# A mixture of experts, dense and then sparse: gathers issued one block earlier, the last six tiles routed as one batch, an accumulator's pool closed inside the last step, and gate scaling at other points

## The chip, the cores and the metric

The kernel runs on one core of a Trainium2 chip. The metric is the time of one execution on the device, in microseconds (us): 2072.86 us is the median of three runs of the kernel before. The engines are named PE (TensorE), DVE (VectorE), ACT (ScalarE), POOL (GpSimd) and SP (SyncE, which only issues transfers and register work here). Each engine executes its own list of instructions in order; waits between engines go by semaphores.

## What is computed

Three parts, all in float32: linear attention over 4 x 8 heads of 576 positions, a dense mixture of experts whose gate is balanced by eight Sinkhorn rounds, and a sparse mixture in which each of 2304 rows goes to one of eight experts.

```
# x: [2304, 512] from the attention
logits = x @ w_gate;  P = exp(logits - logits.max())
for _ in range(8):                       # Sinkhorn
    P /= P.sum(1, keepdims=True) + 1e-9
    P /= P.sum(0, keepdims=True) + 1e-9
    P *= N / E
x = sum(P[:, e:e+1] * (relu(x @ w1[e]) @ w2[e]) for e in range(8))
# sparse: the nearest expert by cosine
logits = normalize(x) @ normalize(expert_emb).T / tau
probs = softmax(logits);  idx = argmax(logits, axis=1)
out[idx == e] = probs[idx == e, e] * (relu(x[idx == e] @ w1b[e]) @ w2b[e])
```

## The kernel before

A product in float32 is made of three float32r matmuls: each operand is split into a high part (a cast) and a low part (the difference), and high x high, high x low and low x high are summed. The casts are mostly ACT's (L328, L374, L456, L926), the differences DVE's or POOL's (L329, L457, L927).

**Stage 1** (to about 290 us) is the attention. **Stage 2** (to about 1753 us) is the dense mixture, 24 steps: an expert e and a block bi of 768 rows (`ORDER`). A step has two groups g, halves of the hidden features. A group is 14 products (`p1_group`, matmuls L447 to L449 into psA, a Strassen-like scheme with seven products for each of two halves j) and then six tiles of the second layer (`p2_tile`, matmuls L668 to L670 into psD), whose results DVE adds into `acca` and `accb`, scaled by the gate. psA has four places. In a half, ACT copies the first product to tu (L469), and later casts h1h (L456, from tv) and h0h (L456), from which DVE makes h1l and h0l (L457). A place of psA comes free when its low part is made.

The work that is laid beside this is placed by hand. A group's 14 products and 6 tiles are its **ticks** 0 to 19. `at_tick(step, g, tick, fn)` puts a function behind a tick; ticks above 19 in the lists of the last steps mean the next group. Placed so are: `w1_tasks(e, g)`, which prepares w1 of an expert (six functions: casts on ACT and subtractions on POOL by `wpiece`, L328 and L329, with POOL's sums L345, L350, L354 and L360 between them); `w2_task`; the routing of the sparse mixture; and the first loads of stage 3. The gate (`gate_logits`) and its Sinkhorn rounds (`sinkhorn`) are generators in a list of hooks; `hook()` advances one of them by a piece. Before, that happens behind each odd tick, from step 0 on behind every one. A Sinkhorn round ends in column sums: DVE makes cs (L650), PE sums over the partitions (L653).

**Routing.** A batch of three tiles of 128 rows goes through `route_a` (squares, transposes L715), `route_l` (logits L725), `route_b` (the best expert on DVE, from L733), `route_c` (ranks, L752 and L753), `route_s`, `route_d` (slot numbers, L768 to L774), `route_w` (weight, and the write of the rows to the DRAM table x2d, L784) and `route_i`: one scatter by POOL for each tile, which writes the row numbers to the tables ids (L788). There are three tables, one for each place in a batch; a scatter waits for the landing of the scatter before it into the same table. Batches 0 and 3 (named by their first tile) lie in step 22, 6 and 9 in step 23, and the last six tiles, which come last out of the accumulator `accb`, are batches 12 and 15.

**Stage 3** is a loop over 22 blocks of 128 places (`second`), each of one expert. `load_ids(i)` loads a block's row numbers (SP: table reads L877 to L879 and three transfers idr from ids, L890), `gather(i)` adds them up (POOL, L897 to L899) and gathers the rows xgs (POOL, L901) into one of two places; `tx` transposes them (L935, ACT's xth L938, DVE's xtl L939 and gt L941), `p1` multiplies by w1 (L955 to L957), `th_` transposes h (L970), `p2` multiplies by w2 (L988 to L990), and the output is scattered by POOL (L994). `wcond` loads a quarter of an expert's matrix where the expert changes (SP, L906), and `wsplit` makes its parts: the casts on ACT (L926), for the last quarter of w2 on POOL (L924), and the low parts on DVE (L927). The first `NEARLY` blocks are known after twelve tiles (`first_blocks`), the others after all (`other_blocks`, a generator).

## Time and profile before

| | us |
|---|---|
| runs | 2067.79, 2072.86, 2074.79 |
| median | 2072.86 |
| the profiled execution, its own time | 2069.92 |
| its span, first to last instruction | 2067.9 |
| PE busy | 2017.4 (98%) |
| DVE busy | 1101.6 (53%) |
| ACT busy | 723.9 (35%) |
| POOL busy | 584.1 (28%) |

The mean granted clock of TensorE is 0.994 of full speed. The profiled execution lies 2.94 us below the median, and its span leaves 2.0 us outside. A share of busy time is a mean over the three stages; what matters is where an engine waits and for what, so the rows below are cut by stretches. A group's line reads "line engine operation output<-input, count | busy us, mean ns | idle time before it and what ended it"; a wait's line "us in total, times, longest".

### The profile page before, as it was taken

Reading aid. Unit: us, or ns where it says so; the run is one execution under the profiler, and the core shown is the slowest. Engines: PE = TensorE matmul, PEld = TensorE weight load, DVE = VectorE, ACT = ScalarE, POOL = GpSimd, SP = SyncE. Lnnn points to the kernel's source line nnn. Section 1 sums busy time; section 2 is a strip of 40 time slices with the busy share of each in tenths; the row PEclk is TensorE's granted clock in tenths of the full one; section 3 lists DMA queues with packets and bytes.
Section 4 is the critical chain, followed back from the end, with each engine's and each line's share of the span. In section 5 each row is a group of like instructions: output and inputs, shape, how many; then the busy total and the mean of one; then the engine's idle time right before and its main releaser. Section 6 shows DMA issues by size and latency. Waiting matters only on the chain.

```text
span 2067.9 us, 28848 instructions
## 1 busy us (share of the span) xinstructions
PE 2017.4 (98%) x10947; PEld 1814.6 (88%) x10947; DVE 1101.6 (53%) x1994; ACT 723.9 (35%) x1331; POOL 584.1 (28%) x482
## 2 busy tenths in 40 slices
PE   9999999999999999999999999999999999799898
PEld 8999888888988998998998998998998988687776
DVE  6766443654444444444444444444444546888886
ACT  5566433321231122113212311321231223687775
POOL 1246452420050034006102400420050102456553
PEclk9999999999999999999999999999999999999999
DMA  3344343112213111221302222112212537252851
GB/s 115 113 142 168 112 166 122 42 42 107 107 62 127 74 54 61 107 107 42 125 31 100 82 107 107 41 57 91 107 62 107 44 106 113 56 204 78 308 189 43
DMA packets 76671, 208.32 MB, mean 101 GB/s; under 512 B 18272, under 2 KB 37984, under 8 KB 76530
## 3 DMA queue, kind: packets, MB, share of 16 engines
q1 hardware_dynamic: 72434, 195.94, 29.0%
q0 software_dynamic: 4096, 10.51, 1.6%
q8 instruction: 87, 1.43, 0.3%
q14 instruction: 54, 0.44, 0.1%
HBM read 230.00 MB, written 31.99 MB: 127 GB/s over the span
## 4 chain that ended last, share of the span: by engine, by line
PE 79%; DVE 6%; DMA 4%; POOL 4%; issue 3%; ACT 2%; SPq 1%; POOLq 0%; DVEq 0%; ACTq 0%
PE psD L668 12%; PE psD L669 12%; PE psD L670 12%; PE psA L447 11%; PE psA L449 11%; PE psA L448 11%; PE psD L197 3%; DMA idr<-ids 2%; POOL xgs L901 2%; DVE s2l L927 2%; DVE s1l L927 1%; PE psB L168 1%; PE psC L168 1%; DMA rw<-in_moe_w 1%; POOL s2h L924 1%
## 5 line engine op out<-in xcount | busy, mean ns | idle before, releaser
L329 POOL TENSOR_TENSOR wA<-raw,wA 128x512 fp32r<-128x512 f32 x48 | 60.9, 1295 | 805.2 <-ACT wA L328 805.2
L679 DVE SCALAR_TENSOR_TENSOR acca<-psD,Pm,acca 128x512 f32<-128x512 f32 x168 | 126.2, 751 | 280.5 <-PE psD L670 279.4
L668 PE MATMUL psD<-w2h,h0h 128*128 128x512 f32 x576 | 225.7, 392 | 0.5 <-DVE accb L679 0.5
L669 PE MATMUL psD<-w2h,h0l 128*128 128x512 f32 x576 | 224.4, 390 | 0.6 <-DVE h0l L457 0.6
L669 PE MATMUL psD<-w2h,h1l 128*128 128x512 f32 x576 | 224.4, 390 | 0.0
L670 PE MATMUL psD<-w2l,h0h 128*128 128x512 f32 x576 | 224.3, 389 | 0.0
L668 PE MATMUL psD<-w2h,h1h 128*128 128x512 f32 x576 | 224.1, 389 | 0.0
L670 PE MATMUL psD<-w2l,h1h 128*128 128x512 f32 x576 | 224.1, 389 | 0.0
L469 ACT COPY tu<-psA 128x384 f32<-128x384 f32 x96 | 46.0, 479 | 446.5 <-PE psA L449 446.5
L447 PE MATMUL psA<-xT,wS 128*128 128x384 f32 x576 | 194.6, 338 | 0.0
L448 PE MATMUL psA<-xT,wS 128*128 128x384 f32 x576 | 192.6, 334 | 0.0
L449 PE MATMUL psA<-xT,wS 128*128 128x384 f32 x576 | 192.5, 334 | 0.0
L456 ACT ACTIVATE h1h<-tv 128x384 fp32r<-128x384 f32 x96 | 50.4, 525 | 264.6 <-DVE tv L461 264.6
L457 DVE SCALAR_TENSOR_TENSOR h0l<-psA,h0h 128x384 fp32r<-128x384 f32 x192 | 106.5, 555 | 62.2 <-ACT h0h L456 61.9
L456 ACT ACTIVATE h0h<-psA 128x384 fp32r<-128x384 f32 x192 | 94.4, 491 | 112.8 <-DVE psA L461 105.9
L679 DVE SCALAR_TENSOR_TENSOR accb<-psD,Pm,accb 128x512 f32<-128x512 f32 x84 | 63.1, 751 | 132.6 <-PE psD L670 121.0
L447 PE MATMUL psA<-xB,wA 128*128 128x384 f32 x384 | 129.9, 338 | 0.0
L927 DVE TENSOR_TENSOR s2l<-rw,s2h 128x1024 fp32r<-128x1024 f32 x88 | 106.3, 1251 | 43.2 <-POOL s2h L924 37.7
L448 PE MATMUL psA<-xB,wA 128*128 128x384 f32 x384 | 129.2, 336 | 0.0
L449 PE MATMUL psA<-xB,wA 128*128 128x384 f32 x384 | 129.0, 336 | 0.0
L669 PEld LDWEIGHTS psD<-w2h,h1l 128*128 128x128 f32 x576 | 108.1, 188 | 23.4 <-DVE h1l L457 0.9
L670 PEld LDWEIGHTS psD<-w2l,h0h 128*128 128x128 f32 x576 | 108.1, 188 | 22.6
(293 smaller groups left out, 4836.0 us busy)
## 6 DMA issues: line engine op xcount, KB each, us to landing
rw<-in_moe_w SPq DMA_DIRECT2D x176, 512.0 KB
xT<-xpd SPq DMA_DIRECT2D x56, 768.0 KB
raw<-in_moe_w SPq DMA_DIRECT2D x64, 512.0 KB
xB<-xpd SPq DMA_DIRECT2D x42, 768.0 KB
xpd<-xT SPq DMA_DIRECT2D x12, 768.0 KB
xpd<-xB SPq DMA_DIRECT2D x9, 768.0 KB
v<-in_v SPq DMA_DIRECT2D x8, 715.0 KB
rk<-in_kT SPq DMA_DIRECT2D x32, 128.0 KB
```

The source lines that it names most:

```text
L197: T.matmul(ps[:, off:off + w], eq[:, sg, h_, ci * P:(ci + 1) * P], kvz[:, h_, sg, o:o + w], start=(sg == 0), stop=(sg == 1))
L329: eng.tensor_tensor(out=t[:, 1], in0=src, in1=f32(t[:, 0]), op=ALU.subtract)
L447: T.matmul(bank, w[:, 0, j, k, :], x[:, 0, k, :], start=start and k == 0, stop=False, skip_group_check=True)
L448: T.matmul(bank, w[:, 0, j, k, :], x[:, 1, k, :], start=False, stop=False, skip_group_check=True)
L449: T.matmul(bank, w[:, 1, j, k, :], x[:, 0, k, :], start=False, stop=stop and k == 1, skip_group_check=True)
L456: A.activation(out=hh[:, j, ts_], in_=src, func=AF.Relu)
L457: V.scalar_tensor_tensor(out=hl[:, j, ts_], in0=src, scalar=0.0, in1=f32(hh[:, j, ts_]), op0=ALU.max, op1=ALU.subtract)
L668: T.matmul(ps, hh[:, j, ts_], wh[:, ws], start=(hv == 0 and j == 0), stop=False)
L669: T.matmul(ps, hl[:, j, ts_], wh[:, ws], start=False, stop=False)
L670: T.matmul(ps, hh[:, j, ts_], wl[:, ws], start=False, stop=(hv == 1 and j == 1))
L679: V.scalar_tensor_tensor(out=o, in0=ps, scalar=Pm[:, t, e:e + 1], in1=o, op0=ALU.mult, op1=ALU.add)
L927: V.tensor_tensor(out=lo, in0=r, in1=f32(hi), op=ALU.subtract)
```

## The change

1. In `second`, `load_ids` and `gather` are for block i + 3 and not i + 2: the first stands at the head of the iteration, the second behind p2 of the block before. `gather(2)` and `gather(3)` move into the last step of stage 2 (ticks 37 and 39), `gather(4)` into the first blocks.
2. The last six tiles are one batch of six (`n = 6`), with tiles and the two PSUM results widened; two scatters go to each ids table.
3. The pool of `acca` (m1, through `st.close()`) closes at tick 19 of the last step's first group, and not after the loop. `w2_first` then makes the first two quarters of the first block's w2 at ticks 23 and 30, inside the last step; before, they were made in `w2_this(0)` of stage 3. The pool wp2 stays open, and four of seven places for w2 lie in it.
4. The hooks go by a table `PLACES` for steps 2 and 3, and by ticks 0, 2, 4, 6 otherwise; the gate's and Sinkhorn's generators enter at tick 19 of the step before.
5. `w1_tasks` of expert 1 moves in step 2 from ticks 13 to 18 of group 0 to ticks 0 to 5 of group 1 (first half of the features) and from 13 to 14 (second half); its w2 tasks go from 4 and 8 to 8 and 12, and in step 3 from 6 and 10 to 8 and 11. Other experts keep their ticks.
6. The batches of the routing lie at other ticks: 0 and 3 wider apart in step 22, 6 begins at the end of step 22, 9 ends one p2 tile earlier; `route_first`, `load_ids`, `gather(0)` and `gather(1)` go from ticks 16, 17, 18, 19 to 12, 15, 16, 17.
7. Small tiles share tags (ci, nb, cum, prev, ei, ri, fl).

```diff
-    live["wp2"] = st.enter_context(tc.tile_pool(name="wp2", bufs=1, reuse_waits="tile"))
+    live["wp2"] = top.enter_context(tc.tile_pool(name="wp2", bufs=1, reuse_waits="tile"))
...
-            n = RB
+            n = NTL - NA if t0 >= NA else RB
...
-            pool, tags, bufs = live["m2l"], ("wsh", "wsl"), 7
+            pool, tags, bufs = (live["m2l"], ("wsh", "wsl"), 3) if j < 3 else (live["wp2"], WP2[j - 3], 1)
...
+    def early_second():
+        st.close()
+        live["m2l"] = top.enter_context(tc.tile_pool(name="m2l", bufs=1, reuse_waits="tile"))
+
+    def w2_first(c):
+        wsplit(0, 2, c)
+        wcond(1, 2, c)
...
-            at_tick(step, 0, 0 if step else filled[0], partial(hooks.append, gate_logits(bi)))
+            at_tick(*((step - 1, 1, 19) if step else (0, 0, filled[0])), partial(hooks.append, gate_logits(bi)))
             if step == NB - 1:
-                at_tick(step, 0, 0, partial(hooks.append, sinkhorn()))
+                at_tick(step - 1, 1, 19, partial(hooks.append, sinkhorn()))
         if step % NB == NB - 1 and e + 1 < E:
-            w1_at(step, 0, e + 1, 13)
-            at_tick(step, 1, 4, w2_task(e + 1, 0))
-            at_tick(step, 1, 8, w2_task(e + 1, 2))
-            w1_at(step, 1, e + 1, 13)
-            at_tick(step + 1, 0, 6, w2_task(e + 1, 1))
-            at_tick(step + 1, 0, 10, w2_task(e + 1, 3))
+            w1_at(e + 1, 0, step, *((1, 0) if e == 0 else (0, 13)))
+            for i, c in ((8, 0), (12, 2)) if e == 0 else ((4, 0), (8, 2)):
+                at_tick(step, 1, i, w2_task(e + 1, c))
+            w1_at(e + 1, 1, step, 1, 14 if e == 0 else 13)
+            for i, c in ((8, 1), (11, 3)) if e == 0 else ((6, 1), (10, 3)):
+                at_tick(step + 1, 0, i, w2_task(e + 1, c))
...
+    PLACES = {(NB - 1, 0): (0, 2, 4, 6, 8, 10, 12, 14, 15, 16, 17, 18, 19), (NB - 1, 1): (8, 11, 15, 17, 19), (NB, 0): (1, 4, 7, 10)}
...
-    route_at(NSTEP - 1, 6, ((0, 1, 2), (2, 3, 4), (6, 10, 8, 11, 12, (12, 12, 12))))
-    route_at(NSTEP - 1, 9, ((4, 5, 6), (6, 7, 8), (12, 14, 13, 15, 15, (15, 15, 15))))
-    last = [(16, route_first)] + [(17, partial(load_ids, i)) for i in range(NEARLY)]
-    last += [(18, partial(gather, 0)), (18, partial(load_raws, 2, (0, 1))), (19, partial(gather, 1)), (29, partial(load_raws, 2, (2,))), (33, start_second)]
+    route_at(NSTEP - 2, 6, ((36, 37, 38), (37, 38, 39), (41, 46, 42, 48, 48, (48, 48, 48))))
+    route_at(NSTEP - 2, 9, ((41, 43, 45), (43, 45, 47), (49, 53, 50, 54, 54, (54, 54, 54))))
+    last = [(12, route_first)] + [(15, partial(load_ids, i)) for i in range(NEARLY)]
+    last += [(16, partial(gather, 0)), (16, partial(load_raws, 2, (0, 1))), (17, partial(gather, 1)), (29, partial(load_raws, 2, (2,))), (19, early_second), (23, partial(w2_first, 0)), (30, partial(w2_first, 1)), (33, start_second)]
...
+    last += [(37, partial(gather, 2)), (39, partial(gather, 3))]
+    tail = route_steps(NA, (36, 37, 38, 39, 41, 43), (37, 38, 39, 40, 42, 44), (45, 47, 46, 48, 49, range(50, 56)))
...
-            if i + 2 >= NEARLY and i + 2 < i1:
-                load_ids(i + 2)
+            early = i + 3 > NEARLY
+            if early and i + 3 < i1:
+                load_ids(i + 3)
             p1(i)
             if i + 1 < i1:
                 w1_next(i, range(4), partial(next, ob, None))
-            if i + 2 < i1:
-                gather(i + 2)
             relu(i)
             if i + 1 < i1:
                 tx(i + 1)
             w2_this(i, partial(next, ob, None))
...
             if i > i0:
                 p2(i - 1, 0)
                 p2(i - 1, 1)
+            if i + 3 < i1:
+                gather(i + 3)
```

Where instructions move, two places matter. The first is ACT in step 2, at the end of group 0 and the start of group 1. L673 copies the result of a p2 tile; wA and wS are parts of w1 of expert 1, raw is their float32 source; tu, h1h and h0h belong to the first products of group 1. Before:

```order
411 L328 CAST wS_1_0_4392<-raw_3481 128x512 [waits Pool_49]
412 L673 COPY acca<-psD_4396 128x512 [waits PE_49]
413 L328 CAST wS_1_0_4411<-raw_3481 128x512 [waits Pool_49]
414 L673 COPY acca<-psD_4414 128x512 [waits PE_49]
415 L328 CAST wS_1_0_4433<-raw_3527 128x512
416 L673 COPY acca<-psD_4437 128x512 [waits PE_49,Activation_49]
417 L328 CAST wS_1_0_4451<-raw_3527 128x512 [waits Pool_49]
418 L673 COPY acca<-psD_4458 128x512 [waits PE_49,Activation_49]
419 L469 COPY tu<-psA_4481 128x384 [waits PE_49]
420 L456 ACTIVATE h1h<-tv 128x384 [waits DVE_49,Activation_49]
421 L456 ACTIVATE h0h<-psA_4481 128x384 [waits PE_49,Activation_49]
```

and now:

```order
412 L469 COPY tu<-psA_4467 128x384 [waits PE_49]
413 L328 CAST wA_1_0_4476<-raw_3481 128x512
414 L328 CAST wA_1_0_4479<-raw_3481 128x512
415 L328 CAST wA_1_0_4490<-raw_3527 128x512
416 L328 CAST wS_1_0_4503<-raw_3481 128x512 [waits Pool_49]
417 L456 ACTIVATE h1h<-tv 128x384 [waits DVE_49,Activation_49]
418 L328 CAST wS_1_0_4518<-raw_3481 128x512 [waits Pool_49]
419 L456 ACTIVATE h0h<-psA_4467 128x384 [waits PE_49,Activation_49]
420 L328 CAST wS_1_0_4529<-raw_3527 128x512
421 L456 ACTIVATE h1h<-psA_4494 128x384 [waits DVE_49]
422 L328 CAST wS_1_0_4542<-raw_3527 128x512 [waits Pool_49]
423 L456 ACTIVATE h0h<-psA_4507 128x384 [waits DVE_49]
```

The casts have moved from beside the copies L673 into the products of group 1, so that h1h and h0h now stand behind casts that wait for POOL.

The second is ACT in step 23 (the last), at the start of group 1: tu, h1h and h0h of its products, and s2h_0, the high part of the first quarter of w2 for stage 3, cast from rw_0. Before:

```order
994 L469 COPY tu<-psA_14720 128x384 [waits PE_49]
995 L456 ACTIVATE h1h<-tv 128x384 [waits DVE_49,Activation_49]
996 L456 ACTIVATE h0h<-psA_14720 128x384 [waits PE_49,Activation_49]
997 L456 ACTIVATE h1h<-psA_14737 128x384 [waits DVE_49]
998 L456 ACTIVATE h0h<-psA_14746 128x384 [waits DVE_49]
999 L469 COPY tu<-psA_14782 128x384 [waits PE_49]
1000 L456 ACTIVATE h1h<-tv 128x384 [waits DVE_49]
1001 L456 ACTIVATE h0h<-psA_14782 128x384 [waits PE_49]
```

and now:

```order
994 L469 COPY tu<-psA_14724 128x384 [waits PE_49]
995 L456 ACTIVATE h1h<-tv 128x384 [waits DVE_49,Activation_49]
996 L923 CAST s2h_0_14760<-rw_0_14665 128x1024 [waits DMAHW7_49,DMAHW2_49,DMAHW1_49]
997 L456 ACTIVATE h0h<-psA_14724 128x384 [waits PE_49,Activation_49]
998 L456 ACTIVATE h1h<-psA_14741 128x384 [waits DVE_49]
999 L456 ACTIVATE h0h<-psA_14750 128x384 [waits DVE_49]
1000 L469 COPY tu<-psA_14791 128x384 [waits PE_49]
1001 L456 ACTIVATE h1h<-tv 128x384 [waits DVE_49]
1002 L923 CAST s2h_1_14829<-rw_1_14667 128x1024 [waits DMAHW0_49]
```

A cast that waits for transfers (DMAHW) has come in ahead of the first h0h. Where its source's load, rw_0, stands on SP is seen in the list of SP now (idr_14517 is the first block's, idr_14641 the fifth's; ids_83 to ids_85 are the three tables, and DMASW marks a wait for a POOL transfer, here a scatter):

```order
355 L886 DMA idr_14517<-ids_83 128x1 [waits DMAHW0_49,DMASW1_49]
...
357 L886 DMA idr_14517<-ids_84 128x1 [waits DMAHW1_49,DMASW2_49]
...
359 L886 DMA idr_14517<-ids_85 128x1 [waits DMAHW2_49,DMASW3_49]
...
379 L886 DMA idr_14579<-ids_83 128x1 [waits DMAHW6_49]
...
403 L886 DMA idr_14641<-ids_83 128x1 [waits DMAHW4_49]
...
405 L886 DMA idr_14641<-ids_84 128x1 [waits DMAHW5_49]
...
407 L886 DMA idr_14641<-ids_85 128x1 [waits DMAHW6_49]
...
409 L902 DMA rw_0_14665<-in_moe_w 128x1024 [waits DMAHW7_49,PE_49]
...
411 L902 DMA rw_1_14667<-in_moe_w 128x1024 [waits DMAHW0_49,PE_49]
```

The load of rw_0 stands behind the five blocks' fifteen loads of idr, as it did before; what is new is the cast that waits for it among the products.

## Rows read from the trace of the kernel before

**Rows 1.** The page's first part: busy time of each engine, its share of the span, and its instructions.

```profile
PE 2017.4 (98%) x10947; PEld 1814.6 (88%) x10947; DVE 1101.6 (53%) x1994; ACT 723.9 (35%) x1331; POOL 584.1 (28%) x482
```

**Rows 2.** Busy time by stretch in stage 3 (start:end, length, then busy time and instructions of PE, weight loads, DVE, ACT and POOL, granted clock, DMA share, GB/s).

```profile
1859.00:1904.00 45.00, 43.45 (x210) 35.60 (x211) 39.12 (x43) 33.52 (x43) 24.67 (x21) 1.00 0.15 43
1904.00:1947.00 43.00, 36.80 (x179) 30.01 (x178) 35.39 (x40) 30.39 (x39) 24.42 (x21) 1.00 0.84 302
```

**Rows 3.** The matmuls of line 970 (transposes of h) in stage 3 into psD, four to a block: duration least/median/greatest in ns, first and last start. First all of the regular blocks, then those of the second block alone.

```profile
L970 PE MATMUL psD<-ident,hr x76: 270/272/273, 1814.8 to 2051.4; 128*128 128x128 f32 x76
...
L970 PE MATMUL psD<-ident,hr x4: 272/272/273, 1827.0 to 1827.4; 128*128 128x128 f32 x4
```

**Rows 4.** 1809 to 2051 us: the wait of PE (us in total, times, longest), and the group of DVE's splits of w2 (count, busy us and mean ns, idle time before them and what ended it).

```profile
PE psA L935 <- DMA xgs<-x2d,idt: 12.1, 10, 3.2
...
L927 DVE TENSOR_TENSOR s2l<-rw,s2h 128x1024 fp32r<-128x1024 f32 x75 | 89.6, 1237 | 40.7 <-POOL s2h L924 37.7 <-ACT s2h L926 3.0
```

**Rows 5.** The chain of work in one calm block, 1855 to 1872 us, in order of time: start, length, what.

```profile
1855.54 1.00 POOL xgs L901
1856.54 1.07 POOL s2h L924
...
1861.61 1.96 DMA idr<-ids
```

**Rows 6.** The gathers (line 901) from 1809 to 2060 us: time of the issue on POOL, and from issue to landing.

```profile
L901 POOL DMA_INDIRECT xgs<-x2d,idt x17: 997/1683/3789, 1812.5 to 2028.0; - x17
...
DMA to landing us min/median/max: 3.4/6.2/9.3
```

**Rows 7.** Two stretches of 5 us with busy DMA engines, columns as in rows 2.

```profile
1742.60:1747.60 5.00, 5.00 (x30) 4.33 (x29) 1.88 (x2) 1.28 (x4) 0.00 (x0) 1.00 0.93 309
1925.00:1930.00 5.00, 2.46 (x13) 2.15 (x14) 5.00 (x6) 3.43 (x6) 0.11 (x1) 1.00 1.05 386
```

**Rows 8.** What PE waited for from 392 to 434 us (step 2 of stage 2).

```profile
PE psC L653 <- DVE cs L650: 5.4, 5, 1.3
```

**Rows 9.** Preparing w1 of expert 1, 404 to 425 us: the casts on ACT, what they waited for, and the subtractions on POOL (first and last start).

```profile
L328 ACT CAST wS<-raw x4: 615/620/625, 412.8 to 421.9; 128x512 fp32r<-128x512 f32 x4
L328 ACT CAST wA<-raw x3: 612/621/622, 406.9 to 408.0; 128x512 fp32r<-128x512 f32 x3
L328 ACTq EVENT_SEMAPHORE  x1: 17/17/17, 417.4 to 417.4; - x1
...
  POOL raw L354: 4.0, 1
...
L329 POOL TENSOR_TENSOR wS<-raw,wS x4: 1284/1290/1294, 413.5 to 422.6; 128x512 fp32r<-128x512 f32 x4
```

**Rows 10.** The second group of products of the last step, from 1716 us: the first product's matmuls, the copy tu, the casts h0h, and the matmuls of p2 that follow.

```profile
L447 PE MATMUL psA<-xB,wA x8: 334/334/339, 1716.5 to 1728.5; 128*128 128x384 f32 x8
...
L469 ACT COPY tu<-psA x1: 481/481/481, 1717.8 to 1717.8; 128x384 f32<-128x384 f32 x1
...
L456 ACT ACTIVATE h0h<-psA x3: 491/493/493, 1722.0 to 1729.2; 128x384 fp32r<-128x384 f32 x3
...
L668 PE MATMUL psD<-w2h,h0h x4: 389/389/389, 1731.1 to 1734.5; 128*128 128x512 f32 x4
```

**Rows 11.** PE's longest wait from 1600 to 1753 us, and a stretch of it with the granted clock (columns as in rows 2).

```profile
PE psC L725 <- DVE lg L733: 2.1, 1, 2.1
...
1685.00:1692.00 7.00, 5.57 (x30) 5.57 (x31) 2.17 (x11) 2.43 (x6) 0.00 (x0) 0.76 0.00 0
```

**Rows 12.** The scatters to ids (line 788) of tiles 6 to 8, then of tiles 9 to 11 with POOL's wait ahead of the second, time from issue to landing, and the writes of x2d (line 784).

```profile
L788 POOL DMA_INDIRECT ids<-tokid,si x3: 961/962/1037, 1698.9 to 1701.5; - x3
...
DMA to landing us min/median/max: 14.6/14.6/14.6
...
L788 POOL DMA_INDIRECT ids<-tokid,si x3: 960/961/1032, 1707.2 to 1716.3; - x3
L788 POOLq EVENT_SEMAPHORE  x1: 17/17/17, 1704.1 to 1704.1; - x1
...
DMA to landing us min/median/max: 15.2/15.2/15.2
...
L784 SPq DMA_DIRECT2D x2d<-acca x2: 370/370/371, 1700.7 to 1707.4; - x2
```

**Rows 13.** p2 in step 23 (first start of its matmuls), a calm p2, the loads of idr on SP from the third one on, and the loads of rw behind them.

```profile
L668 PE MATMUL psD<-w2h,h0h x24: 387/389/497, 1698.7 to 1750.1; 128*128 128x512 f32 x24
...
L668 PE MATMUL psD<-w2h,h0h x12: 389/389/389, 1460.2 to 1474.5; 128*128 128x512 f32 x12
...
L890 SPq DMA_DIRECT2D idr<-ids x13: 332/333/339, 1728.2 to 1741.2; - x13
...
L906 SPq DMA_DIRECT2D rw<-in_moe_w x4: 96/333/333, 1741.8 to 1743.9; - x4
```

**Rows 14.** The start of stage 3: what PE waited for from 1753 to 1810 us, busy time from 1790 to 1815 (columns as in rows 2), the casts s2h on ACT, and a routing operation of DVE.

```profile
PE psA L956 <- DVE gt L941: 7.0, 1, 7.0
...
1790.00:1815.00 25.00, 17.98 (x75) 14.44 (x74) 24.76 (x38) 13.48 (x18) 11.68 (x9) 0.80 0.34 88
...
L926 ACT CAST s2h<-rw x3: 1037/1044/1044, 1759.2 to 1761.1; 128x1024 fp32r<-128x1024 f32 x3
...
L769 DVE TENSOR_TENSOR sl<-sl,oh 128x24 f32<-128x24 f32 x2 | 0.4, 184 | 0.1
```

More of the change, by code (lines that the diff above doesn't have):

```diff
@@ L679, in p2_tile @@
             V.scalar_tensor_tensor(out=o, in0=ps, scalar=Pm[:, t, e:e + 1], in1=o, op0=ALU.mult, op1=ALU.add)
-    ohc = c0.tile([P, 5, E], BF16, name="ohc")
+    ohc = c0.tile([P, 7, E], BF16, name="ohc")
     V.memset(ohc[:, 0, :], 0.0)
@@ L700, in route_a @@
         r = batch(t0)
-        if t0 == NA and i == 0:
-            live["m2r"].tile([P, 16], F32, name="m2pad")
         x2 = acc(t0 + i)[:, 0:DM]
         if t0 == NA:
+            if i == 0:
+                live["m2r"].tile([P, 16], F32, name="m2pad")
             scr = live["m2r"].tile([P, DM], F32, tag=f"hT{'hl'[i % 2]}", bufs=2, name=f"scr{t0 + i}")
-        elif t0 > NA:
-            if i == 0:
-                r["scr"] = hp.tile([P, 2 * DM], F32, tag="h1l", name=f"scr{t0}")
-            scr = r["scr"][:, i % 2 * DM:(i % 2 + 1) * DM]
         else:
@@ L749, in route_c @@
         n, oh = r["n"], r["oh"]
-        r["pr"] = psum("B", [P, 4, E])
+        r["pr"] = psum("C" if t0 == NA else "B", [P, 6, E])
         o = r["pr"][:, 0:n, :].rearrange("p n e -> p (n e)")
@@ L778, in route_w @@
         n = r["n"]
-        se = sm.tile([P, 4], F32, tag="se", name=f"se{t0}")[:, 0:n]
+        se = sm.tile([P, 6], F32, tag="se", name=f"se{t0}")[:, 0:n]
         V.tensor_reduce(out=se, in_=r["lg"], axis=AX.X, op=ALU.add)
@@ L787, in route_i @@
         si = rt[t0]["si"]
-        G.indirect_dma_start(out=ids[i], out_offset=bass.IndirectOffsetOnAxis(si[:, i:i + 1], 0), in_=tokid[:, t0 + i:t0 + i + 1], in_offset=None)
+        G.indirect_dma_start(out=ids[i % RB], out_offset=bass.IndirectOffsetOnAxis(si[:, i:i + 1], 0), in_=tokid[:, t0 + i:t0 + i + 1], in_offset=None)
     meta = c0.tile([1, 3, NBLK], I32, name="meta")
@@ L797, in counts @@
         T.matmul(ps, onesb, ohc[:, at_, :], start=True, stop=True)
-        ci = sm.tile([1, E], I32, name=f"ci{add}")
+        ci = sm.tile([1, E], I32, tag="ci", name=f"ci{add}")
         V.tensor_scalar_add(ci, ps[0:1, :], float(add))
         V.tensor_single_scalar(ci, ci, 7, op=ALU.logical_shift_right)
-        nb = sm.tile([1, E], F32, name=f"nb{add}")
+        nb = sm.tile([1, E], F32, tag="nb", name=f"nb{add}")
         V.tensor_copy(nb, ci)
@@ L908, in build @@
     w2t = {}
-    n_w1 = [0]
+    n_w = {1: 0, 2: 0}
+    WP2 = tuple((f"w2h{c}", f"w2l{c}") for c in (0, 2, 1, 3))
     PAIRS = (("wA11_1", "wA12_1"), ("wA22_1", "wS1_1"), ("wS3_1", "wS4_1"))
@@ L1025, in build, with w1_at @@
     w2_task(0, 2)()
-    def w1_at(step, g, e, first_tick):
+    def w1_at(e, g, step, half, first_tick):
         for i, fn in enumerate(w1_tasks(e, g)):
-            at_tick(step, g if e else 0, first_tick + i, fn)
-    w1_at(0, 1, 0, 13)
+            at_tick(step, half, first_tick + i, fn)
+    w1_at(0, 1, 0, 0, 13)
     at_tick(0, 1, 4, w2_task(0, 1))
@@ L1088, in build @@
             for _ in gen:
-                if tick % 2 or step == 0:
+                if hookable(step, g, tick):
                     hook()
@@ L1095, in build @@
                 p2_tile(e, bi, g, tt)
-                if tt % 2 or step == 0:
+                if hookable(step, g, tick):
                     hook()
@@ L1101, in build @@
     assert not sched, sched.keys()
[L1103 to L1104 removed]
     load_raws(2, (3,))
[L1106 removed]
+    tail = iter(tail[7:])
     def rhook(n):
@@ L1133, in w1_next, with w2_this @@
                     wcond(i + 2, 1, c)
-        def w2_this(i, hook):
-            for c in range(4):
+        def w2_this(i, hook, cs=range(4)):
+            for c in cs:
                 wsplit(i, 2, c)
@@ L1144, in second @@
         if i0 == 0:
+            p1(0, (2, 2, 1, 1))
+            first_w1(1, (3,))
+            relu(0)
             rhook(1)
-            p1(0)
-            first_w1(1, (3,))
+            w2_this(0, no, range(2, 4))
+            p1(1, (0, 1))
             rhook(2)
-            gather(2)
-            relu(0)
-            w2_this(0, partial(rhook, 2))
-            rhook(1)
-            p1(1, (1, 1, 1, 1))
+            w1_next(1, range(2))
             th_(0, 0)
-            rhook(1)
+            rhook(3)
             th_(0, 1)
-            rhook(2)
             relu(1)
-            w1_next(1, range(1))
             p2(0, 0)
-            rhook(1)
             tx(2)
-            w1_next(1, range(1, 2))
-            rhook(2)
+            gather(4)
+            w1_next(1, range(2, 3))
             p2(0, 1)
-            gather(3)
-            rhook(4)
+            rhook(3)
+            next(ob)
             th_(1, 0)
             th_(1, 1)
-            w1_next(1, range(2, 4))
+            w1_next(1, range(3, 4))
             next(ob)
@@ L1185, in second @@
             w2_this(i, partial(next, ob, None))
-            if i == NEARLY - 3:
+            if not early:
                 for _ in ob:
                     pass
+                load_ids(i + 3)
             if i > i0:
@@ L1203, in build @@
         prime(NALW)
+        load_ids(NALW + 2)
+        gather(NALW + 2)
         for c in range(4):
```

52 lines of the change are left out of this document (25 added, 27 removed).

## The prediction

> **What bounds the kernel now.** I read the busy times first, then the busy times by stretch, then PE's waits and the chain of waits inside the stretches that are not full. PE is busy 98% of the span [rows 1], so a change earns something only where it takes away one of PE's few waits, and it costs something wherever it makes a new one, whatever another engine saves. The time goes by PE's order of work, and every other engine matters at the points where PE waits for it.
>
> In stage 3 PE is busy 43.45 of 45 us from 1859 to 1904 and 36.80 of 43 from 1904 to 1947, at clock 1.00 in both [rows 2]: that is waiting. A block's period can be read from the first transposes of h (L970) of two blocks: 12.2 us from 1814.8 to 1827.0, where PE has no wait [rows 3]. Those transposes, four to a block, run from 1814.8 to 2051.4 for 19 blocks, so 18 periods took 2051.4 - 0.3 - 1814.8 = 236.3 us, where 18 x 12.2 = 219.6 would do. **Some 16 us** are lost there. The waits say to what: PE waited 10 times, 12.1 us, for gathered rows (xgs), and DVE 37.7 us for POOL's cast s2h [rows 4]. The chain shows why [rows 5]: gather (1.00 us), cast s2h behind it on POOL, split s2l on DVE, only then SP's loads of the next block's numbers (idr from ids, 1.96), POOL's address sums, and the next gather behind them. This circle is passed once per block and takes longer than 12.2 us.
>
> **Gathers.** The loads of ids move from two blocks ahead to three, to the head of the iteration. POOL's own order (gather, s2h, output scatter, address sums) stays. The circle now spans two periods: it has 24.4 us. A gather is then held by its place alone, which tx of two blocks before frees; it lands in 3.4 to 9.3 us [rows 6], and more than a period lies between that and its use. So the 16 us can go down to what is next late. That is the loading of weights at changes of expert: 1904 to 1947 moved 302 GB/s x 43 us = 13.0 MB [rows 2], and a 5 us window shows that 386 GB/s are possible [rows 7]; 13.0 MB at 386 take 33.7 us, under three periods (36.8). DVE is busy 39.12 of 45 us [rows 2], under 11 us per block. Bounds: -16 (all of it) and 0 (the same time comes back as waits for weights); I take **-14 us**, near the upper end, because calm blocks run at the full rate already [rows 3].
>
> The gather's issue of 1.00 to 3.79 us [rows 6] bears on a rule: the Trainium skill (SBUF — State Buffer, on the trap of DVE and DMAs issued by GpSimd) says that such descriptors can't be written while DVE holds the port that they share. By it a gather would stay long wherever DVE casts; no row here shows the port itself. What it would do is rival 3.
>
> **Sinkhorn in other places.** PE waits five times, 5.4 us, for the column sums' input cs [rows 8]. The new places put a p2 tile (2.7 us) or several products between two rounds at most points; the first round still has too little ahead of it. I keep about 3 of such waits as left, with the weight loads' share: **-3 us** (0 to -5.4).
>
> **Preparing w1 of expert 1.** These seven casts on ACT and seven subtractions and four sums on POOL move from p2 tiles of step 2, group 0, into the first products of group 1. POOL is the slow one: between the first cast and the second wS cast lie L329 three times, L345, L329, L350 and L354, and ACT waits for POOL; the first wA cast is at 406.9, the second wS cast at 417.4, the last at 421.9 [rows 9]. Before, only the copies L673 stand behind these casts. Now h0h does: order on ACT is tu, casts, h1h, second wS cast, h0h. A group of products, by the last step's calm one, starts at 1716.5, has its tu (L469, 0.48) 1.3 us later, its first h0h (0.49) at 1722.0, and its 14 products take until 1731.1, 1.04 each [rows 10]. With the chain, the second wS cast starts 1.8 + 10.5 = 12.3 us after the group's start, ends at 12.9, h0h at 13.4, h0l (0.55) at 13.9. The eighth product needs the place in psA that this h0l frees, and would start at 7 x 1.04 = 7.3 us: PE stands for 6.6. The fourth wS cast, 4.5 us after the second, holds the next h0h and costs some 1.4 more. **+8 us**; bounds 0 (POOL well ahead) and 11 (half clock behind it, as below).
>
> **Routing re-placed.** Around the routing in steps 22 and 23 PE waits for DVE and ACT, longest 2.1 us for the logits lg, and right there, 1685 to 1692, it was busy 5.57 of 7 us at clock 0.76 [rows 11]: 1.4 us idle and 0.24 x 7 = 1.7 of clock. Shorter waits of the same kind lie at five other places, some 3 us by the lines before and after them. Wider places give most of it back: **-5 us** (-1 to -6.5).
>
> **Split of w2 in the last step.** New is a wait: ACT's cast s2h_0 stands at the fourth product of group 1 in step 23, ahead of h0h. It needs rw_0 of w2, whose load is on SP behind all 15 loads of idr, and the first three of these wait for the scatters to ids of the last batch. Count from P, the start of p2 in group 0, 1698.7 before [rows 13]. The last batch's first scatter went out at 1707.2, P + 8.5; one p2 tile earlier it is P + 5.7. Three scatters need P + 7.7. They land 14.6 and 15.2 us after issue while x2d is written (issued 1700.7 and 1707.4) [rows 12]. Lower bound for the third landing: P + 7.7 and 5.1, the wait of the next scatter for a landing ahead of the writes (1698.9 to 1704.1) [rows 12], P + 12.8; upper: P + 7.7 + 15.2 = P + 22.9. Middle: P + 17.9. Then the remaining 12 loads of idr with their table reads: 1728.2 to 1741.2 [rows 13], 13.0 us; then rw_0 goes out 0.6 later, at 1741.8, and some 3 us go by until 512 KB are there (three such loads moved in the 5 us at 309 GB/s [rows 7]). So rw_0 is there at P + 34.5. Cast (1.04 [rows 14]), h0h, s2l or h1l, and h0l bring PE's next product some 2.9 us later: P + 37.4. PE comes to the eighth product of group 1 at P + 16.3 (six tiles of p2 in a calm step: 1460.2 to the last h0h at 1474.5, and the 9 of 12 matmuls of that tile that are left, 0.23 each [rows 13]) + 7.3 = P + 23.6. **+14 us**, bounds 9 and 19. Before, the same cast came at 1759.2 [rows 14], and no wait for it is shown. PE's stand of 7.0 us in 1790 to 1815 left a clock of 0.80 there [rows 14]: half speed for 10 of the 25 us, of which 5.5 lay behind the stand and cost 2.7. I add **+2.5**.
>
> The landing bears on a rule too. Here the scatters that were issued during the writes took 14.6 and 15.2 us [rows 12]. The Trainium skill (DMA: Bandwidth & Descriptors, on queues, rings and completion order) says that a DMA engine takes turns between queues, packet by packet. By that rule a scatter, in another queue than the write, would not wait for the whole write, the landing would be the lower bound, and this term 9 and not 14; the trace speaks against it.
>
> **Last six tiles as one batch.** 1790 to 1815 is bound by DVE (24.76 of 25 us busy) and PE's largest single wait, 7.0 us for gt, is there [rows 14]. One batch less takes some 19 operations of 0.18 us from DVE (by L769), 3.4 us, and the two splits of w2 that moved out are 2 x 1.24 (mean of the later ones [rows 4]): 5.9 us. A wait of hTl in the first block's p2 stays. **-4.5 us** (0 to -7). New tags, shared buffers and the fewer rows of ohc's copy lie beside PE's work: 0.
>
> **Sum.** -14 - 3 - 5 - 4.5 + 8 + 14 + 2.5 = **-2 us** from the profiled execution, 2069.9, which is 3 us below the median of 2072.9. On the median's scale **2071 us**. A measurement of this kernel tells a difference of some 0.3%, 6.2 us, from none.
>
> **Rivals.**
> 1. *The cast s2h_0 doesn't hold PE* (rw_0 there by P + 21, because the scatters land early and SP's 15 loads come closer together). For it: SP has little else in that stretch. Against: 13.0 us of SP between idr loads are read from the trace. -14 and -2.5 fall away: 2071 - 16.5 = 2054.5. With rival 2 as well 2046.5.
> 2. *POOL's chain doesn't hold h0h in step 2.* For it: raw is there long before. Against: POOL's operations are in one queue and 1.29 us each. 2063.
> 3. *The gathers bring nothing* (the slower side): POOL's gather and s2h stay late, or s2h waits for weights, so DVE's 37.7 us stay; it decides if a gather takes 3.79 us in most blocks, since s2h stands behind it. For it: that wait was POOL's, and its order is unchanged. Against: POOL is busy 24.67 of 45 us [rows 2]. 2071 + 14 = 2085.
> 4. *The last step's stall at its upper bound and clock loss behind both stalls*: +5 + 4 = 2080.
>
> **How the numbers follow.** Forecast (the moves cancel, 2064 to 2078): 0.37. Rival 1 alone 0.20, with 2 0.08; rival 2 alone 0.09; rival 3 0.14; rival 4 0.12. Faster by over 0.3%: 0.20 + 0.08 + 0.09 + 0.04 of the forecast's = 0.41; slower: 0.14 + 0.12 + 0.02 = 0.28; the rest, 0.31, within. The range takes in rival 1 with part of rival 2 and rival 3: 2049 to 2086; the forecast's own is 2064 to 2078.
>
> **What would show it.** Right: L935 no longer waits for xgs and the 18 periods take about 222 us; in step 2, group 1, PE waits about 7 us with ACT waiting for POOL at a wS cast; in step 23, group 1, PE waits over 8 us with ACT waiting for the load of rw; L956 waits less than 4 us for gt. Wrong: no wait of PE in one of the two groups (rival 1 or 2), or DVE still waits over 20 us for s2h (rival 3).

## The result and the profile after

The changed kernel takes 2088.5 us (median of six runs) against 2072.5 in the same session: ratio **1.0075**, 95% interval 1.0058 to 1.0093, some 16 us slower. Forecast was 2071, range 2049 to 2086. The profiled execution has a span of 2087.1 us, 19.2 more than before's (this one lay 0.8 us above its median, before's below). From the routing on, lines of the changed kernel have numbers 3 or 4 lower than before's: L932 is before's L935.

First what PE waited for in the whole program (us in total, times, longest):

```profile
PE psA L447 <- DVE h0l L457: 23.9, 4, 18.0
PE psA L953 <- DVE gt L938: 5.4, 1, 5.4
PE psD L987 <- DVE hTl L971: 3.6, 2, 3.4
PE psC L653 <- DVE cs L650: 3.5, 3, 1.7
PE psD L668 <- DVE accb L679: 2.4, 2, 1.9
PE psC L721 <- DVE lg L729: 2.0, 1, 2.0
...
PE psA L932 <- DMA xgs<-x2d,idt: 1.2, 1, 1.2
```

The wait for gathered rows, 12.1 us in [rows 4], is down to 1.2. The wait for cs went from 5.4 [rows 8] to 3.5, the one for gt from 7.0 [rows 14] to 5.4. New are 23.9 us for h0l, 18.0 of them at once, and 2.4 for accb. Where they lie, by stretch (columns as in rows 2):

```profile
388.10:411.30 23.20, 17.54 (x90) 16.64 (x89) 10.18 (x21) 9.01 (x17) 15.84 (x12) 0.85 0.15 47
...
1709.80:1732.00 22.20, 19.12 (x75) 14.54 (x75) 10.62 (x41) 1.58 (x4) 3.59 (x4) 0.92 0.61 124
1732.00:1766.30 34.30, 16.33 (x86) 15.98 (x85) 9.73 (x16) 5.64 (x10) 3.67 (x11) 0.75 0.28 66
1787.00:1848.60 61.60, 52.43 (x252) 42.71 (x252) 46.64 (x88) 36.73 (x53) 22.98 (x20) 0.92 0.26 53
```

The first is the products of step 2, group 1, with the granted clock at 0.85; the second and third are step 23's first p2 and the last 14 products, which took 14.6 us before [rows 10] and 34.3 now. The fourth, the start of stage 3, took 61.8 us before.

**Stage 3.** The transposes of h, the gathers, and DVE's splits of w2 from 1848 us on, to be set beside [rows 3, 4, 6]:

```profile
L967 PE MATMUL psD<-ident,hr x76: 270/272/273, 1848.6 to 2070.6; 128*128 128x128 f32 x76
...
L897 POOL DMA_INDIRECT xgs<-x2d,idt x17: 1673/1679/3814, 1846.3 to 2039.5; - x17
...
DMA to landing us min/median/max: 4.0/5.1/8.4
...
L924 DVE TENSOR_TENSOR s2l<-rw,s2h 128x1024 fp32r<-128x1024 f32 x70 | 93.0, 1386 | 5.3 <-ACT s2h L923 3.3 <-POOL s2h L921 2.0
```

18 periods now take 2070.6 - 0.3 - 1848.6 = 221.7 us and not 236.3; DVE waits 2.0 us for POOL's s2h and not 37.7, though a gather's issue takes at least 1.67 us now and s2h stands behind it as before.

**Step 2, group 1** (products from 388.1): ACT's casts with the wait for POOL, and the first h0h:

```profile
L328 ACT CAST wS<-raw x4: 608/618/622, 395.6 to 405.0; 128x512 fp32r<-128x512 f32 x4
L328 ACT CAST wA<-raw x3: 620/622/623, 389.9 to 390.9; 128x512 fp32r<-128x512 f32 x3
...
  POOL raw L354: 3.8, 1
...
L456 ACT ACTIVATE h0h<-psA x1: 483/483/483, 401.0 to 401.0; 128x384 fp32r<-128x384 f32 x1
```

The first h0h is 12.9 us behind the group's start and not 5.5 [rows 10]; PE stood 5.4 us for its low part, until 402.2, where the prediction had 402.1 (388.1 + 14.0).

**Step 23** (first p2 from 1709.8 = P): the last batch's scatters, the fifteen loads of idr, the loads of rw behind them, and ACT's cast with its wait:

```profile
L784 POOL DMA_INDIRECT ids<-tokid,si x3: 955/961/1036, 1720.4 to 1723.0; - x3
...
L886 SPq DMA_DIRECT2D idr<-ids x15: 332/333/339, 1728.6 to 1751.2; - x15
...
L902 SPq DMA_DIRECT2D rw<-in_moe_w x2: 332/332/333, 1751.9 to 1752.6; - x2
...
L923 ACT CAST s2h<-rw x1: 1044/1044/1044, 1755.7 to 1755.7; 128x1024 fp32r<-128x1024 f32 x1
its engine sat idle before it (us, times) until:
  DMA rw<-in_moe_w: 18.1, 1
```

This is the chain that the prediction drew, later at each point: scatters from P + 10.6 (forecast P + 5.7), the third idr load at 1738.3, P + 28.5 (P + 17.9), the load there at P + 45.8 (P + 34.5). PE came to it later too, at P + 30.6 (P + 23.6): from P to the next group are 22.2 us and not 16.3, and it is the ninth product that has to wait, not the eighth (in step 2 as well).

### The profile page after: what moved, and what is told of

Its sections match the earlier page's. It is cut to its first block, busy times and chain, and to the rows that moved or that the text cites. A ratio compares the mean times of both kernels' runs of the same rounds, so it can differ in the third digit from the quotient of the medians.

```text
span 2087.1 us, 28816 instructions
## 1 busy us (share of the span) xinstructions
PE 2024.5 (97%) x10945; PEld 1821.9 (87%) x10945; DVE 1108.9 (53%) x1976; ACT 721.3 (35%) x1330; POOL 574.0 (28%) x481
## 3 DMA queue, kind: packets, MB, share of 16 engines
q1 hardware_dynamic: 72418, 195.94, 27.1%
## 5 line engine op out<-in xcount | busy, mean ns | idle before, releaser
L447 PE MATMUL psA<-xT,wS 128*128 128x384 f32 x576 | 196.2, 341 | 23.9 <-DVE h0l L457 23.9
L447 PEld LDWEIGHTS psA<-xT,wS 128*128 128x128 f32 x576 | 109.2, 190 | 26.0 <-DVE h0l L457 25.4
L924 DVE TENSOR_TENSOR s2l<-rw,s2h 128x1024 fp32r<-128x1024 f32 x88 | 114.8, 1359 | 30.7 <-ACT s2h L923 28.7
L668 PEld LDWEIGHTS psD<-w2h,h0h 128*128 128x128 f32 x576 | 108.3, 188 | 25.0 <-DVE accb L679 3.2
L447 PE MATMUL psA<-xB,wA 128*128 128x384 f32 x384 | 129.6, 337 | 0.0
L448 PE MATMUL psA<-xB,wA 128*128 128x384 f32 x384 | 128.8, 336 | 0.0
```

The costliest lines, as they stand in the source:

```text
L447: T.matmul(bank, w[:, 0, j, k, :], x[:, 0, k, :], start=start and k == 0, stop=False, skip_group_check=True)
L448: T.matmul(bank, w[:, 0, j, k, :], x[:, 1, k, :], start=False, stop=False, skip_group_check=True)
L668: T.matmul(ps, hh[:, j, ts_], wh[:, ws], start=(hv == 0 and j == 0), stop=False)
L924: V.tensor_tensor(out=lo, in0=r, in1=f32(hi), op=ALU.subtract)
```

## The experiments

Ratios are to the kernel before on the same chip, with 95% intervals; 0.001 is 2.07 us. "Kernel 4", or a 4 in parentheses, is the kernel of experiment 4; "theory" and "rival" are those of the expectation that stands above the measured time. "Half clock" is a granted clock of 0.5, 1.2 GHz and not 2.4.

**1. The load of w2 ahead of the loads of idr** (in the changed kernel):

```diff
-    last += [(16, partial(gather, 0)), (16, partial(load_raws, 2, (0, 1))), ...
+    last = [..., (15, partial(load_raws, 2, (0, 1)))] + [(15, partial(load_ids, i)) ...]
```

> The changed kernel with the loads of the first two quarters of w2 issued on SP ahead of the fifteen loads of idr instead of behind them; the casts s2h stay at ticks 23 and 30. Theory (the 18.1 us wait of PE in the last step is the wait for that load, which stands behind idr): the wait goes, PE waits under 1 us there, and the time falls by 16 to 19 us against the changed kernel, to about 2071. Rival (the wait only covers lateness that would show anyway at the start of stage 3, where the gathers and DVE's list are not ready sooner): the wait goes, but L953 or L932 wait longer at the start of stage 3 and the time falls by under 8 us, to 2081 or more.

Measured 1.0018 (1.0007 to 1.0030), 2076.3 us: 12 us below the changed kernel, between theory and rival. The start of stage 3 took only 1.8 us longer, so the rival is wrong; but 5 us of the wait stayed. The load, the cast, and the stretch (columns as in rows 2):

```profile
L902 SPq DMA_DIRECT2D rw<-in_moe_w x2: 595/640/685, 1721.1 to 1722.2; - x2
...
L923 ACT CAST s2h<-rw x1: 1044/1044/1044, 1741.5 to 1741.5; 128x1024 fp32r<-128x1024 f32 x1
...
  DMA rw<-in_moe_w: 4.9, 1
...
1720.00:1742.00 22.00, 19.49 (x92) 17.11 (x91) 5.69 (x9) 1.54 (x3) 2.28 (x3) 0.95 0.99 166
```

Issued at 1721.1, the load was there at 1741.4: 20 us where the late one of the changed kernel took 3.7, in a stretch with the DMA engines 99% busy at 166 GB/s, under the write of x2d (issued 1720.3) and four loads for w1.

**2. The two splits at ticks 37 and 38 instead of 23 and 30** (in the changed kernel):

```diff
-(23, partial(w2_first, 0)), (30, partial(w2_first, 1))
+(37, partial(w2_first, 0)), (38, partial(w2_first, 1))
```

> The changed kernel with the first two splits of w2 at ticks 37 and 38 instead of 23 and 30; nothing else differs. Theory (with the loads ahead of idr 5 us of the wait stayed, because the load of w2 then shared the DMA engines with the write of x2d; with the cast behind the load's usual landing nothing waits): PE has no wait over 1 us in the products of the last group, and the time falls by 17 to 19 us against the changed kernel, to about 2070. Rival (the two splits then lie where DVE and ACT are wanted for the first blocks): the wait goes, but the start of stage 3 gets 4 us longer or more, 2074 or above.

Measured 0.9979 (0.9966 to 0.9991), 2067.4 us: the theory. The last products take 14.6 us again and PE has no wait there (columns as in rows 2):

```profile
1730.20:1744.80 14.60, 14.60 (x86) 14.60 (x85) 8.59 (x16) 3.99 (x9) 3.09 (x8) 1.00 0.31 35
```

The place of two casts was worth 20 us and turns the change from slower to faster.

**3. w1 and w2 of expert 1 at their old ticks** (in the changed kernel):

```diff
-            w1_at(e + 1, 0, step, *((1, 0) if e == 0 else (0, 13)))
+            w1_at(e + 1, 0, step, 0, 13)
```

(and the other w1 and the w2 tasks likewise.)

> The changed kernel with w1_tasks and w2_tasks of expert 1 at the ticks of the kernel before. Theory (POOL's chain of sums and subtractions holds h0h in step 2, group 1): PE's wait of 5.6 us and the half clock behind it go, and the time falls by 8 to 11 us, to about 2079. Rival (the Sinkhorn pieces at their new places cost that time, the w1 chain only happens to stand at the same point): PE still waits over 4 us in step 2, group 1, now for cs or h0l, and the time falls by under 4 us.

Measured 1.0052 (1.0033 to 1.0070), 2081.6: some 5 us below the changed kernel by the ratios, whose intervals overlap. The wait for h0l in step 2 is gone, so POOL's chain held it. But from the start of step 2 to the end of step 3's first group the trace has 110.2 us, where before has 106.1 and the changed kernel 114.5. Before, the changed kernel (columns as in rows 2), and PE's waits for cs in kernel 3:

```profile
349.60:455.70 106.10, 100.68 (x510) 87.94 (x509) 60.45 (x138) 33.95 (x63) 37.88 (x27) 1.00 0.16 52
```

```profile
352.00:466.50 114.50, 104.15 (x510) 89.47 (x509) 58.61 (x138) 33.91 (x63) 37.80 (x26) 0.97 0.14 48
```

```profile
PE psC L653 <- DVE cs L650: 5.9, 4, 3.8
```

So 4.1 us are left against before, but they are not the other half of the changed kernel's loss. That kernel waits 3.5 us for cs, 1.7 at the longest; the wait of 3.8 came in when the w2 tasks went back together with w1. The next two experiments show why.

**4. The Sinkhorn pieces alone** (in the kernel before; `PLACES`, `hookable` and the entry at tick 19):

> The kernel before with only the gate's and Sinkhorn's pieces at the changed kernel's places (PLACES and the entry at tick 19 of the step before). Theory (from the kernel with w1 put back, where steps 2 and 3 took 110.2 us against 106.1): 3 to 5 us slower than before, about 2077, with a wait for cs of some 4 us in step 3. Rival (the prediction's term): PE waits less than 3 us for cs and the time is 2 to 4 us below before, about 2070.

Measured 1.0027 (1.0011 to 1.0043), 2076.3: slower, the theory. PE's waits for cs are 5.9 us in place of 5.4, but one of them is 3.8, and half clock for 6.8 us goes with it. The same stretch as in experiment 3 (columns as in rows 2), DVE's multiplication L649 at its end, and POOL's subtraction L376:

```profile
347.40:457.60 110.20, 103.91 (x510) 90.21 (x510) 65.66 (x138) 33.93 (x63) 37.69 (x27) 0.97 0.15 50
...
L649 DVE TENSOR_TENSOR Pm<-Pm,rs x2: 307/1236/2166, 426.1 to 434.6; 128x144 f32<-128x144 f32 x2
...
L376 POOL TENSOR_TENSOR w2l<-raw,w2h x2: 2340/2416/2491, 430.4 to 434.2; 128x1024 fp32r<-128x1024 f32 x2
```

The L649 of 434.6 took 2.17 us instead of 0.31. POOL's L376 had begun at 434.2; both ended at 436.6 to 436.7.

**5. That L376 on DVE instead** (in kernel 4):

```diff
-            (V if e == 0 and c == 0 else G).tensor_tensor(out=lo, ...)
+            (V if (e, c) in ((0, 0), (1, 3)) else G).tensor_tensor(out=lo, ...)
```

> The kernel with only the Sinkhorn pieces at the changed kernel's places, and in it one POOL operation less: the low part of the last quarter of w2 of expert 1 (L376, 2.34 us on POOL, running while DVE's L649 took 2.17 us instead of 0.31) is made by DVE. Theory (POOL's subtraction and DVE's multiplication of two SBUF operands keep each other out, and so cs comes late and PE's wait of 3.9 us brings half clock): L649 takes 0.31 us at that place, PE's wait there falls under 2.5 us though DVE has 1.2 us more to do, the half clock of 6.8 us goes, and the time is 3 to 5 us below the kernel with the pieces alone (2076.3), about 2072. Rival (L649 was long for another reason, its place in DVE's list is what delays cs): L649 stays over 1 us, the wait stays at 3.9 us or grows by 1.2, and the time is within 2 us of 2076.3.

In the stretch, the theory. L649, PE's waits, and the stretch (columns as in rows 2):

```profile
L649 DVE TENSOR_TENSOR Pm<-Pm,rs x2: 307/308/310, 429.2 to 437.7; 128x144 f32<-128x144 f32 x2
```

```profile
PE psC L653 <- DVE cs L650: 4.0, 4, 1.9
```

```profile
350.60:456.20 105.60, 101.23 (x510) 88.02 (x509) 64.74 (x139) 33.89 (x63) 35.27 (x25) 1.00 0.15 52
```

No half clock there, and steps 2 and 3 up to the same point take 105.6 us, not 110.2. The time doesn't show it: 1.0016 (0.9998 to 1.0033), 2077.9 on a chip with before at 2074.2. This profile waits 19.3 us for xgs, kernel 4's 12.7, in stage 3, which the edit doesn't touch: the old circle of gathers differs by that much between these two executions. By time alone it is inconclusive.

The changed kernel doesn't have this meeting of L649 and L376. Its w2 tasks in step 3 stand at ticks 8 and 11 and not 6 and 10, its last two L376 begin at 444.4 and 448.0, and no L649 takes over 1.03 us:

```profile
L649 DVE TENSOR_TENSOR Pm<-Pm,rs x8: 307/310/1026, 375.5 to 448.0; 128x144 f32<-128x144 f32 x8
```

So what the Sinkhorn pieces cost alone is not what they cost in the changed kernel. A kernel with the new places of w1 and w2 and the old ones of Sinkhorn was not run.

**6. route_first, the loads of ids and the first gathers at their old ticks** (in the changed kernel):

```diff
-    last = [(12, route_first)] + [(15, partial(load_ids, i)) for i in range(NEARLY)]
+    last = [(16, route_first)] + [(17, partial(load_ids, i)) for i in range(NEARLY)]
...
```

> The changed kernel with route_first, load_ids, gather(0) and gather(1) of the last step at ticks 16 to 19 again (12, 15, 16, 17 in the changed kernel). Theory (the thirty small DVE operations of first_blocks stand ahead of the additions into accb and of the last batch's slot numbers): PE's two waits for accb (2.4 us) and the half clock behind them go, the last batch's scatters go out some 3 us earlier after the start of p2, and the wait for w2's load shrinks by about as much: 5 to 8 us less than the changed kernel, about 2082. Rival (the scatters' landing behind the write of x2d and the rw loads sets the time, not their issue): the accb waits go but the wait for rw stays at 18 us or grows, and the time falls by under 4 us or not at all.

Measured 1.0043 (1.0025 to 1.0061), 2080.2: the theory. The waits for accb go, the scatters are issued 3.2 us earlier (P + 7.4, with P = 1706.8), and the wait behind rw is 14.8 us:

```profile
L784 POOL DMA_INDIRECT ids<-tokid,si x3: 954/958/1036, 1714.2 to 1716.8; - x3
...
DMA to landing us min/median/max: 10.2/10.8/12.0
...
PE psA L447 <- DVE h0l L457: 14.8, 1, 14.8
```

**7. The routing alone** (in the kernel before: the ticks of batches 0 to 9 and of route_first to gather(1)):

> The kernel before with only the ticks of the routing batches 0 to 9, of route_first, load_ids, gather(0) and gather(1) of the changed kernel. Theory (first_blocks ahead of the additions into accb and of the last batch): two waits for accb of 2.4 us in the last step, steps 22 and 23 up to the last group's first product take 120 to 121 us instead of 116.3, and the time is 3 to 5 us above before, about 2077. Rival (the prediction's term): the waits for lg and the half clock go and the time is 4 to 6 us below before, about 2068.

Measured 1.0014 (1.0001 to 1.0028), 2075.1: slower, the theory. Waits from 1603 to 1740 us, and the stretch of steps 22 and 23 up to the last products (columns as in rows 2):

```profile
PE psC L725 <- DVE lg L733: 2.0, 1, 2.0
PE psD L668 <- DVE accb L679: 1.9, 1, 1.9
PE psD L668 <- ACT h0h L456: 1.1, 1, 1.1
```

```profile
1603.10:1723.90 120.80, 114.79 (x623) 102.64 (x622) 57.57 (x175) 29.72 (x70) 15.87 (x16) 0.97 0.31 88
```

Before it is 116.3:

```profile
1600.20:1716.50 116.30, 112.46 (x622) 101.38 (x621) 57.51 (x175) 30.05 (x70) 14.72 (x16) 0.99 0.53 75
```

The wait for lg is still there, in step 22, and two new ones came. Of the 4.5 us, 2.2 are more waiting (length less PE's busy time) and 2.3 are the clock.

**8. The gathers alone** (in the kernel before: `load_ids(i + 3)` and `gather(i + 3)` as in the diff):

> The kernel before with only the gathers and the loads of ids one block earlier in the loop of stage 3 (gather(4) follows gather(3) in the first blocks). Theory (the circle gather, s2h, s2l, load of ids, gather held every block): PE no longer waits for xgs in the loop, the regular period is 12.23 to 12.28 us at every block, and the time falls by 13 to 16 us against the kernel before, to about 2058. Rival (part of that gain came from the other changes, such as a later start of the loop that left weights and gathers more time): blocks at expert switches still take 13 to 15 us, and the time falls by under 8 us.

Measured **0.9933** (0.9913 to 0.9952), 2057.6: the theory. Every period from 1829.8 us to the last but one is 12.23 to 12.28, at changes of expert too.

**9. What is left with before's tables for stage 2** (the changed kernel with those tables, the splits at 37 and 38):

> The changed kernel with the kernel before's tables for all of stage 2 (Sinkhorn pieces, w1 and w2 of expert 1, routing batches 0 to 9, route_first and first gathers), and the first two splits of w2 at ticks 37 and 38, in the p2 tiles of the last group. What is left of the change: gathers one block earlier, the last six tiles as one batch, the early closing of the pool. Theory (the batch of six earns next to nothing, since DVE is as full at the start of stage 3 as it was): within 3 us of the kernel that has the gathers alone (2057.6). Rival (the prediction's term of -4.5 us, which the stalls of the last step only hide): 2052 to 2054. Second rival (the six tiles in one batch cost, since every scatter and block number waits for all six): 2061 or more.

Measured 0.9933 (0.9915 to 0.9952), 2058.5, the same as the gathers alone: the batch of six, with the early closing and the two splits moved ahead, earns nothing that can be measured. PE's waits from 1734 to 1820 us:

```profile
PE psA L953 <- DVE gt L938: 5.4, 1, 5.4
PE psD L987 <- DVE hTl L971: 3.4, 1, 3.4
PE psC L721 <- ACT scr L712: 2.0, 1, 2.0
```

These have taken the place of 7.0 for gt and 2.6 for sl before. Its profile had half clock for 13.7 us around the wait for lg that ends at 1684.6, before's 3.4 around the same wait. This suggested the last two.

**10 and 11. No wait for lg in the last step** (on kernels 8 and 9):

```diff
-    route_at(NSTEP - 1, 9, ((4, 5, 6), (6, 7, 8), ...
+    route_at(NSTEP - 1, 9, ((6, 7, 8), (8, 9, 10), ...
```

> The kernel before with the gathers one block earlier, and the transposes and logits of batch 9 two ticks later (6, 7, 8 and 8, 9, 10), so that DVE has read batch 6's logits before PE writes the next ones to the same place. Theory (the wait of 2.2 us for lg in the last step and the half clock of 3.4 to 13.7 us behind it are one loss): no wait for lg there, clock 1.00 from 1670 to 1720, and 3 to 5 us below the kernel with the gathers alone, about 2054. Rival (the wait moves to the ranks, L752, since batch 9's best expert is then found later): the same time within 2 us.

> The kernel with the gathers, the batch of six and the late split of w2, on the tables of the kernel before, and the transposes and logits of batch 9 two ticks later. Theory: as in the kernel beside it the wait for lg and the half clock go, which in this kernel's profile was 13.7 us long; 4 to 6 us below 2058.5, about 2053.5, within 3 us of the kernel beside it. Rival (the batch of six earns what the prediction said, hidden until now by the clock): over 3 us below the kernel beside it, 2050 or less.

Measured 0.9907 (0.9887 to 0.9928), 2055.4, and 0.9905 (0.9884 to 0.9927), 2055.8. The first products of step 23 in kernels 9, 8 and 10 (columns as in rows 2):

```profile
1669.70:1701.60 31.90, 29.55 (x159) 28.51 (x158) 11.25 (x34) 11.52 (x27) 0.88 (x1) 0.79 0.00 1
```

```profile
1671.80:1698.90 27.10, 24.74 (x159) 23.89 (x158) 11.26 (x34) 11.53 (x27) 0.88 (x1) 0.94 0.00 2
```

```profile
1669.00:1694.00 25.00, 23.21 (x159) 22.33 (x158) 11.26 (x34) 11.43 (x27) 0.88 (x1) 1.00 0.00 1
```

The work is the same; it took 31.9 and 27.1 us by the clock alone, and 25.0 with 0.6 us less of waiting besides. In kernel 10 PE's longest wait there is 1.5 us (for ACT), and the clock stayed at 1.00. The intervals of 8 and 10 overlap by 0.0015, so the gain of 2 to 5 us is likely and not shown by time. Kernels 10 and 11 take the same time, so the batch of six earns nothing without that wait either. Kernel 10 is the fastest here, 0.9% below before and 33 us below the changed kernel.

## Why the prediction was wrong

The mechanisms of both stalls and of the gathers were right, and the direction was lost in the sum. The step that failed most is the routing: -5 was forecast and +4.6 came. The two other terms put down as gains, Sinkhorn and the last six tiles, gave less than forecast, and both stalls cost more. By stretches of the two profiles (us), with the single experiment beside it:

| term | forecast | by stretch | alone |
|---|---|---|---|
| gathers | -14 | -14.6 | -13.9 (8) |
| Sinkhorn pieces and w1 of expert 1 | -3 + 8 | +8.4 | +5.6 (4) and +4.8 (against 3) |
| routing | -5 | +4.6 | +2.9 (7) |
| split of w2, clock | +16.5 | +19.7 | +20 (against 2) |
| last six as one batch | -4.5 | -1.4 | 0 (9) |
| stage 1 (to the first product), not touched | 0 | +2.4 | differs by 5 between executions |

The stretches come to +19.1 where the forecast had -2. Of these 21 us, routing is 9.6, Sinkhorn with w1 3.4, the split of w2 3.2, the last six 3.1 and stage 1, where executions differ, 2.4. The last column comes from ratios with intervals of some 3 to 4 us to either side, and of 4 to 5 where it is a difference of two ratios, so the +4.8 is not clear of noise by time.

1. *Gathers*: right, in size too. The circle was the limit, and weights came in time at every change of expert. Rival 3 fell: POOL's gather is no shorter than before (its median issue is 1.68 us in both), and s2h is not late, since the gather no longer waits for ids.
2. *Routing re-placed* is the step that failed most: "Wider places give most of it back". It looked only at waits that exist, and not at what is moved in ahead of other work on DVE. first_blocks, 19 small operations (not thirty, as the expectation of experiment 6 has it) from 1713.9 to 1717.1, now stands ahead of the last low parts of the products, the additions into accb and the last batch's slot numbers (6). Its first and last operation:

```profile
1713.87 0.14 DVE L795 TENSOR_SCALAR ci<-psC 1x8 int32<-1x8 f32 x1
...
1716.95 0.16 DVE L851 TENSOR_TENSOR taken<-taken,nb 1x8 f32<-1x8 f32 x1
```

And the wait for lg was taken to go where it only moved to step 22. Both cost clock as well: 0.93 there, 0.92 in step 23's first p2.

3. *Sinkhorn*: the number of waits was forecast, not their length. Alone, their sum hardly changed (5.4 to 5.9), and one long wait with half clock cost more than five short ones without (4); what runs on POOL beside a moved piece was not looked at. In the changed kernel, whose w2 tasks had moved too, three waits are left, as the prediction has it, 3.5 us in all: 1.9 less than before, where it said 3. That L649 and L376 do not meet there is luck as far as the prediction goes.
4. *w1*: right in place and to 0.1 us in time. The waits for h0l in the group are 5.7 us, the longest 5.4, in place of 6.6 and 1.4, since the ninth product waits and not the eighth. But a clock of 0.85 over 23.2 us cost 3.5 more, which the prediction had only in its bound. With 1.9 less for cs and some 1 us of short waits that comes to the 8.4.
5. *Split of w2*: right in mechanism, and above its middle: PE waited 18.0 us and 13.8 were forecast, inside the bounds; the clock cost 1.7 (34.3 - 18.0 - 14.6) in place of 2.5. That the wait came so near is in part luck: the load was there 11.3 us later than forecast, and PE came 7.0 us later. Part of both comes from item 2 (6). The landing was between what the trace and the rule said: next to one write the scatters landed after 8.1 us, next to a write and four loads after 8.2, 13.2 and 15.3, neither 5.1 nor, these last three, behind the whole write. The Trainium skill (DMA: Bandwidth & Descriptors, on queues, rings and completion order) has engines take turns between queues; that they landed before the write did (in kernel 1 at 1728.6, 1735.0 and 1738.4, the write at 1740.2) agrees with it, and the lower bound that I tied to it was too low. The batch beside one write and the scatters of kernel 6 (10.2 to 12.0 us) landed 0.2 to 3.3 us behind their write (there at 1713.3 and 1725.9 by the trace), so they don't decide it.
6. *Last six tiles*: 3.4 us less on DVE came out of a list that then stood 6.9 us waiting for PE's logits of six tiles (DVE idle until 1767.2 in kernel 9). DVE was full there before; with one batch it first starves, and from 1767 to 1806 it is busy 30.9 of 39 us (kernel 9). PE's wait for gt stays at 5.4 us, so the sign of less than 4 did not come true; no run shows what holds gt then.

## What to carry to other kernels

A table of places is a set of single bets: cost each place by what stands behind the moved instruction on its in-order engine, and ask for each cast that waits for a load what queue that load stands in. Where a loop has a circle over several engines, issue its slow link one period earlier; that was worth 14 us and needed nothing else. Ask also what runs on the other engines beside the new place: beside one table of w2 the same Sinkhorn pieces made PE wait 5.9 us, beside another 3.5. Sum gains at their lower bound when each rests on the absence of a new wait: here, taken alone, all three such terms came out at or above zero, and with their bounds of 0, -1 and 0 the sum would have been +9.5, of the right sign.
